# Random-feature attention, MLP and capacity-routed experts on one core: accumulator hand-over, low parts kept on chip and load order around the range check

## The chip, the cores and the metric

The kernel runs on one core of a Trainium2 chip, as one program. The metric is the device time of one execution in microseconds (us), taken as the median of several runs. A core has TensorE (PE; its weight loads are listed apart as PEld), VectorE (DVE), ScalarE (ACT), GpSimd (POOL) and SyncE (SP, which here issues most DMA transfers).

## The reference

Three layers follow each other over 2304 tokens (4 batches of 576, 8 heads of 64, so 512 features a token), all in float32:

```python
q_p, k_p = phi(q*scale), phi(k*scale)      # exp(x@omega.T - |x|^2/2 - max) / sqrt(128)
x = (q_p @ (k_p.T @ v)) / (q_p @ k_p.sum(seq) + 1e-6)         # per batch and head
h = x @ w_in; x = (h - tanh(h)) @ w_out                       # 512 -> 2048 -> 512
logits = x @ w_gate                                           # 8 experts
for idx in argsort(-logits.flatten()):                        # greedy, 288 tokens an expert at most
    tok, e = idx // 8, idx % 8
    if assigned[tok] < 0 and counts[e] < 288: assigned[tok] = e; counts[e] += 1
for e in range(8):
    out[assigned == e] = relu(x[assigned == e] @ w1[e]) @ w2[e]   # 512 -> 1024 -> 512
```

## The kernel before, in words

**Precision.** A float32 product is made of three fast matmuls: each operand is split into a high part H and a low part L (line 298 copies the high part, line 303 subtracts it to give the low one), and H·H, H·L and L·H are added in PSUM. The names end in H and L accordingly: `xH`/`xL` the tokens, `gH`/`gL` the hidden values, `iL` and `oL` the low parts of `w_in` and `w_out`, which are kept in DRAM and loaded chunk by chunk (L563).

**Blocks and chunks.** The MLP runs over 6 blocks of 384 tokens. A block has 16 chunks of 128 hidden features: 12 first matmuls a chunk (L601 to L603), a polynomial for h − tanh h on ACT and DVE (L605, L625 to L628), the split into `gH` and `gL`, and 9 second matmuls a chunk (`m2_ops`, L648; below "m2"), three for each of the block's three token tiles, into three accumulators in PSUM, `acc0` to `acc2` (the ring `accr`).

**The last two blocks.** Blocks 4 and 5 go through the first half together, chunk by chunk. Block 5's first matmuls use the same three accumulators as their PSUM room, while block 4's use the four-bank ring `bank`. A shortcut replaces their m2 in the gate: `last_logits` gets the logits from `gH`, `gL` and the precomputed product w_out·w_gate (L719, L721), and L732 and L736/L737 transpose and add them. Block 4's `gH` stay in the place of the used `w_in` chunk (`wi`); its `gL` go to DRAM (L800) and come back for the m2 (L822), through a ring of four slots. Block 5's `gH` and `gL` (`gH5`, `gL5`) stay on chip.

**The range check.** The polynomial holds for a limited range. All engines read one flag (L1464) and branch (L1465); the branch's body, which computes everything again with tanh, is not entered with these inputs. Block 4's m2 for its first three chunks (27 m2) stand ahead of the check, the other 117 behind it, then block 5's 144 (`last_ops`).

**Routing and experts.** Behind the check the capacity search for the experts begins: DVE forms masks (L992 to L996, L1035), PE counts them (nine small matmuls, L1041), DVE decides (L1060, L1062), PE spreads the decision (L1066), and so on, threaded between the m2; L1198 and L1205 give the list of expert 0's tokens, L1161 starts the next expert. Expert 0's tokens are gathered and transposed (L1311); those that lie in the last block are picked by a selection matrix from that block's own results `mH`/`mL` (L1315). Then come the experts' matmuls (L1339 to L1341 by w1, L1358 to L1360 by w2), whose weights are loaded as 512 KB pieces (`wraw`, L1254 and L1257), the high part on ACT, the low part from DRAM (L1266) or by subtraction.

**Order.** A `Plan` object records each operation with its engine, a cost and a due time (`plan.at`), takes its dependences from the buffers that it reads and writes (`op`), and then emits the program engine by engine in the planned order. So an edit of a due time, of a ring of buffers, or of a dependence changes the order on all engines.

## Time and profile before

| what | value |
|---|---|
| median of 3 runs | 907.14 us (904.26 to 910.89) |
| the profiled execution | 907.36 us |
| span of its instructions | 905.5 us |
| TensorE busy | 866.9 us, 96% of the span |
| VectorE, ScalarE, GpSimd busy | 651.0, 467.1, 251.9 us |
| mean granted TensorE clock | 0.980 of full speed |
| DMA traffic | 194.72 MB, 215 GB/s in the mean |

The span runs from the first to the last instruction; 1.86 us of the execution's time lie around it. All positions below are us from the start of the span. The range check lies at 544.5, block 4's last m2 at 582.6, block 5's at 628.1; from there on the experts run. A duration listed for a matmul is from its start to its modelled end; consecutive matmuls overlap, so that their pace is read from their starts.

### The profile page before, as it was taken

The page shows a single profiled execution, that of the slowest core. Times are in us where ns is not written, and L with a number is a line of the kernel's source. Part 1 is how long each engine was busy: PE and PEld are TensorE (multiplying, and loading weights), DVE is VectorE, ACT ScalarE, POOL GpSimd, SP SyncE. Part 2 cuts the span into 40 slices and gives each one's busy share as a digit, 9 for nine tenths or more (in the row PEclk, how much of TensorE's full clock was granted, in tenths as well). Part 3 has the DMA queues.
Part 4 walks back from the last instruction along what each step waited for, and adds up shares of the span by engine and source line. Part 5 has one row for each costly group of instructions (what it writes and reads, how often), then busy time and mean ns, then how long its engine had stood idle before and what let it go on. Part 6 is the DMA issues. An engine that isn't in the chain of part 4 may idle for free. (4 is left out here: it accounts for less than half of the span.)

```text
span 905.5 us, 17561 instructions
## 1 busy us (share of the span) xinstructions
PE 866.9 (96%) x6168; PEld 770.9 (85%) x6168; DVE 651.0 (72%) x1933; ACT 467.1 (52%) x1015; POOL 251.9 (28%) x272
## 2 busy tenths in 40 slices
...
GB/s 245 345 270 270 273 235 282 275 226 224 116 221 166 206 201 225 176 101 111 158 318 259 273 192 176 229 196 132 236 265 260 283 219 232 266 191 278 215 28 26
DMA packets 104364, 194.72 MB, mean 215 GB/s; under 512 B 28369, under 2 KB 42833, under 8 KB 104274
## 3 DMA queue, kind: packets, MB, share of 16 engines
...
## 5 line engine op out<-in xcount | busy, mean ns | idle before, releaser
L601 PE MATMUL bk<-xH,wi 128*128 128x384 f32 x320 | 114.0, 356 | 1.6 <-DVE xt L500 1.3
L648 PE MATMUL acc<-wo,gL 128*128 128x512 f32 x288 | 114.6, 400 | 0.0
L602 PE MATMUL bk<-xL,wi 128*128 128x384 f32 x320 | 107.9, 337 | 0.5 <-DVE xL L303 0.5
L603 PE MATMUL bk<-xH,iL 128*128 128x384 f32 x320 | 107.9, 337 | 0.0
L707 DVE SCALAR_TENSOR_TENSOR lw<-wf,raw 128x512 f32<-128x512 f32 x128 | 105.4, 824 | 2.9 <-POOL wf L704 1.4
L648 PE MATMUL acc<-wo,gH 128*128 128x512 f32 x240 | 100.2, 417 | 0.0
L303 POOL TENSOR_TENSOR gL<-s,gH 128x384 fp32r<-128x384 f32 x52 | 62.0, 1193 | 137.0 <-ACT gH L298 137.0
L648 PE MATMUL acc<-oL,gH 128*128 128x512 f32 x240 | 95.8, 399 | 0.3 <-DVE oL L303 0.3
L438 ACT ACTIVATE phi<-bk,nm 128x128 f32<-128x128 f32 x272 | 76.9, 379 | 36.1 <-DVE nm L441 35.5
L704 POOL TENSOR_TENSOR wf<-oL,wo 128x512 f32<-128x512 f32 x48 | 65.6, 1366 | 70.5 <-DMA oL<-low_wo 65.9
L626 DVE SCALAR_TENSOR_TENSOR s<-s,bk 128x384 f32<-128x384 f32 x80 | 44.0, 550 | 43.7 <-ACT s L625 43.0
L298 ACT ACTIVATE gH<-s 128x384 fp32r<-128x384 f32 x80 | 42.2, 527 | 62.1 <-DVE s L628 46.9
L601 PEld LDWEIGHTS bk<-xH,wi 128*128 128x128 f32 x320 | 60.6, 189 | 7.1 <-issue 1.5
L648 PEld LDWEIGHTS acc<-wo,gL 128*128 128x128 f32 x288 | 54.7, 190 | 12.7
L602 PEld LDWEIGHTS bk<-xL,wi 128*128 128x128 f32 x320 | 60.7, 190 | 3.3 <-DVE xL L303 0.7
L605 ACT ACTIVATE u<-bk 128x384 f32<-128x384 f32 x80 | 39.1, 488 | 43.7 <-PE bk L603 42.5
L603 PEld LDWEIGHTS bk<-xH,iL 128*128 128x128 f32 x320 | 60.4, 189 | 0.0
L441 DVE TENSOR_REDUCE nm<-bk 128x4 f32<-128x512 f32 (+1 forms) x75 | 46.5, 633 | 14.3 <-PE bk L427 13.2
L628 DVE SCALAR_TENSOR_TENSOR s<-s,u 128x384 f32<-128x384 f32 x80 | 52.8, 660 | 1.1
L648 PEld LDWEIGHTS acc<-wo,gH 128*128 128x128 f32 x240 | 45.5, 189 | 6.8
L625 ACT ACTIVATE s<-u,qbias 128x384 f32<-128x384 f32 x80 | 49.3, 616 | 3.8 <-DVE gL L303 1.4
L648 PEld LDWEIGHTS acc<-oL,gH 128*128 128x128 f32 x240 | 45.5, 190 | 6.6 <-DVE oL L303 0.6
...
## 6 DMA issues: line engine op xcount, KB each, us to landing
...
```

Source lines behind the costliest of these rows:

```text
L303: (nc.gpsimd if e == POOL else nc.vector).tensor_tensor(out, in_, high.bitcast(F32), op=OP.subtract)
L438: nc.scalar.activation(ph.t[:, i0 + i, :], pj.t[:, i * M:(i + 1) * M], AF.Exp, bias=nmx.t[:, i0 + i:i0 + i + 1])
L441: plan.op(DVE, 0.1 + 0.125 * n, lambda e, pj=pj, i0=i0, n=n: V.tensor_reduce(nmx.t[:, i0:i0 + n], pj.t[:, :n * M].rearrange("p (i m) -> p ...
L601: nc.tensor.matmul(ph(), piece(iH, c), xH.t[:, c, :], start=(c == 0), stop=False)
L602: nc.tensor.matmul(ph(), piece(iH, c), xL.t[:, c, :], start=False, stop=False)
L603: nc.tensor.matmul(ph(), piece(iL, c), xH.t[:, c, :], start=False, stop=(c == NC - 1))
L625: plan.op(ACT, 0.52, lambda e: nc.scalar.activation(s.t, ut(), AF.Square, bias=qbias), r=[u], w=[s], lag=2.8)
L626: plan.op(DVE, 0.52, lambda e: V.scalar_tensor_tensor(s.t, s.t, QD, ph(), op0=OP.add, op1=OP.mult), r=[p, s], w=[s], lag=3.4)
L628: plan.op(DVE, 0.65, lambda e: V.scalar_tensor_tensor(s.t, s.t, QC, ut(), op0=OP.mult, op1=OP.mult), r=[u, s], w=[s], lag=4.0)
L648: nc.tensor.matmul(acc[t].t, (gL if k == 2 else gH).t[:, c], (oL if k == 1 else oH).t, start=(f == 0 and k == 0), stop=(f == NF - 1 and k ...
L704: plan.op(POOL, 1.45, lambda e: nc.gpsimd.tensor_tensor(w.t, lo.t.bitcast(F32), wo[:, f, :].bitcast(F32), op=OP.add), r=[lo, wbuf["wo", f] ...
L707: x_reads.append(plan.op(DVE, 0.9, lambda e, i=i: nc.vector.scalar_tensor_tensor(scratch.t.bitcast(F32), w.t, 1.0, half(rows[i // 2], i % ...
```

## The change

1. `Plan.op` gets partial reads and writes (`rp`, `wp`): the three or four pieces of `xH`/`xL`, and of the experts' `xgH`/`xgL`, are no longer ordered against each other as whole tiles.
2. Block 5's first matmuls for its last three chunks take their PSUM room from `bank` and no longer from `accr`, and block 4's first m2 wait for block 5's chunk 12 (`freed`) instead of its last chunk.
3. For block 4's last two chunks, 14 and 15 (`NKEEP`), `gL` stays on chip in two new buffers (`gLk0`, `gLk1`), and their `oL` are loaded early into two slots of the ring `xm`. They are the first two chunks behind the check, and accumulation ends at chunk 13 (`end`).
4. Expert 0's weight loads are tied to block 5's loads of `oL` (`turn`, `oloads`), one piece per chunk at the earliest. Three of the eight freed `wi` places go to the experts' low parts, and the slot counts `SLOTS` follow.
5. Block 5's last three chunks (`ALONE`) are done token tile by token tile, so that the tiles end one after the other; the fourth bank of expert 0's transposes takes `acc1`, and `switch3`, which hands the accumulators to the experts, moves behind expert 0.
6. On the path for out-of-range inputs, one ring has one slot less and two buffers are written in one step. These instructions are not executed here.

Where an operation may go to POOL or to DVE, the plan decides anew: of the 32 splits of the experts' w1 that are made ahead of the check (`dw`, L303), POOL has ten instead of six, the last five of them in the place of its last three.

The diff, cut to its core (lines left out give `op` its new parameters, add the ring `keptr` with two tiles, and cast `xm`, which is now stored as the matmuls' type):

```diff
-        for b in w:
+        for b in (*w, *wp):
             if b.ring is not None:
                 o.new.append(b)
                 if not b.writers:
                     b.ring.order.append((o.prio, b))
-            o.deps.update(b.readers)
+            if b in w:
+                o.deps.update(b.readers)
             b.writers.append(o)
-        for b in r:
+        for b in (*r, *rp):
...
-        plan.op(ACT, 0.48, lambda e: copy(e, part(xH), pv()), r=[tp], w=[xH], lag=0.6)
-        plan.op(DVE, 0.6, lambda e: low(e, part(xL), pv(), part(xH)), r=[tp, xH], w=[xL], lag=1.3)
+        o = plan.op(ACT, 0.48, lambda e: copy(e, part(xH), pv()), r=[tp], wp=[xH], lag=0.6)
+        plan.op(DVE, 0.6, lambda e: low(e, part(xL), pv(), part(xH)), r=[tp], rp=[xH], wp=[xL], after=[o], lag=1.3)
...
-        p, u, s = Buf(accr if alone else bank), Buf(gHr if alone else ur), Buf(sr)
+        p, u, s = Buf(accr if alone and f < NF - TPB else bank), Buf(gHr if alone else ur), Buf(sr)
...
-    def m2_ops(f, g, wsp, acc, prev, fine=False):
+    def m2_ops(f, g, wsp, acc, prev, fine=False, end=NF - 1, tiles=range(TPB)):
...
-        for t in range(TPB):
+        for t in tiles:
...
-                                     start=(f == 0 and k == 0), stop=(f == NF - 1 and k == 2), skip_group_check=True)
+                                     start=(f == 0 and k == 0), stop=(f == end and k == 2), skip_group_check=True)
...
+            if f == NF - TPB - 1:
+                freed[:] = flags[-1:]
...
-            gH, gL = Buf(None, wi[:, f, :BLK]), Buf(gLr)
+            stay = f >= NF - NKEEP
+            gH, gL = Buf(None, wi[:, f, :BLK]), None if stay else Buf(gLr)
             gH.readers = list(wbuf["wi", f].readers)
+            if stay:
+                gL, oL = kept.setdefault(f, (Buf(keptr), Buf(xmr)))
+                at, plan.at = plan.at, start[j] + 20.0
+                plan.op(SP, 0.47, lambda e, f=f, oL=oL: nc.sync.dma_start(oL.t.bitcast(F32), lows["wo", f]), w=[oL],
+                        after=[stored_low["wo", f]], nbytes=P * DM * 4)
+                plan.at = at
             hidden_ops(s4, gH, gL)
             lprev4 = last_logits(j, lacc4, f, lprev4, gH, gL)
-            g4[f] = gH, plan.op(SP, 0.47, lambda e, f=f, gL=gL: nc.sync.dma_start(g4l[f], gL.t.bitcast(F32)), r=[gL],
-                                nbytes=P * BLK * 4, lag=6.8)
+            g4[f] = gH, None if stay else plan.op(
+                SP, 0.47, lambda e, f=f, gL=gL: nc.sync.dma_start(g4l[f], gL.t.bitcast(F32)), r=[gL],
...
-        but_last_ops(0, NHERE, start[j] + step[j] * NF + 1.0, 2.0)
-
-    g4, acc4, prev4 = {}, [], [None]
+        for b in kept_bufs() if not general else ():
+            b.left += 1
+        but_last_ops(range(NHERE), start[j] + step[j] * NF + 1.0, 2.0)
+
+    g4, acc4, prev4, freed = {}, [], [None], []
...
-    def but_last_ops(f0, f1, start, step):
-
-        for f in range(f0, f1):
-            plan.at = start + step * f
...
+    kept_bufs = lambda: [b for f in sorted(kept) for b in kept[f]]
+
+    def but_last_ops(chunks, start, step):
+
+        for i, f in enumerate(chunks):
+            plan.at = start + step * i
             gH, st = g4[f]
-            gL = Buf(gLr)
-            plan.op(SP, 0.47, lambda e, f=f, gL=gL: nc.sync.dma_start(gL.t.bitcast(F32), g4l[f]), w=[gL], after=[st],
-                    nbytes=P * BLK * 4)
-            prev4[0] = m2_ops(f, (gH, gL), split_ops("wo", f), acc4, prev4[0] if f else [flags[-1]] * TPB)
-
-    stored, stored4, m5 = [], [], []
+            if st:
+                gL = Buf(gLr)
+                plan.op(SP, 0.47, lambda e, f=f, gL=gL: nc.sync.dma_start(gL.t.bitcast(F32), g4l[f]), w=[gL], after=[st],
+                        nbytes=P * BLK * 4)
+                oH, oL = split_ops("wo", f)
+            else:
+                (gL, oL), oH = kept[f], wbuf["wo", f]
+            prev4[0] = m2_ops(f, (gH, gL), (oH, oL), acc4, prev4[0] if f else freed * TPB, end=NF - NKEEP - 1)
+
+    stored, stored4, m5, oloads = [], [], [], []
+    ALONE = 3
...
+        wsp = []
         for f in range(NF):
             plan.at = start + step * f
-            prev = m2_ops(f, g5[f], split_ops("wo", f), acc, prev, True)
+            wsp.append(split_ops("wo", f))
+            oloads.append(wsp[f][1].writers[-1])
+            if f < NF - ALONE:
+                prev = m2_ops(f, g5[f], wsp[f], acc, prev, True)
         for t in range(TPB):
+            for f in range(NF - ALONE, NF):
+                plan.at = start + step * (NF - ALONE + (f - NF + ALONE + ALONE * t) / TPB)
+                prev = m2_ops(f, g5[f], wsp[f], acc, prev, True, tiles=[t])
+        for t in range(TPB):
+            plan.at = -60.0
             hi, lo = Buf(mHr), Buf(mLr)
             plan.op(ACT, 0.48, lambda e, hi=hi, t=t: copy(e, hi.t, acc[t].t), r=[acc[t]], w=[hi])
             plan.op(DVE, 0.6, lambda e, hi=hi, lo=lo, t=t: low(e, lo.t, acc[t].t, hi.t), r=[acc[t], hi], w=[lo])
...
-    SLOTS = {"wraw": (3, 4), "ewH": (0, 4), "ewL": (1, 11), "xg": (NG - 1, NG - 1), "xgH": (1, 2), "xgL": (1, 2),
+    SLOTS = {"wraw": (3, 4), "ewH": (0, 7), "ewL": (1, 8), "xg": (NG - 1, NG - 1), "xgH": (1, 2), "xgL": (1, 2),
...
-            plan.op(SP, 0.47, load, w=[raw], after=[o], nbytes=P * FX * 4)
+            turn = [] if p else [oloads[min(2 * i + 2, NF - 1)]]
+            plan.op(SP, 0.47, load, w=[raw], after=[o] + turn, nbytes=P * FX * 4)
...
-                plan.op(SP, 0.47, load_low, w=[L], after=[o], nbytes=P * FX * 4)
+                turn = [] if p else [oloads[2 * i + 3]]
+                plan.op(SP, 0.47, load_low, w=[L], after=[o] + turn, nbytes=P * FX * 4)
...
-        plan.at = base + AT_TURN if p else -58.0
         for c in range(NC):
-            tp = Buf(bank3)
+            plan.at = base + AT_TURN if p else -58.0 if c < NC - 1 else AT_LAST + AT_W * NF
+            tp = Buf(accr if c == NC - 1 and not p else bank3)
...
                 o = plan.op(PE, 0.38, others, r=xg, w=[tp])
+                plan.at = AT_LAST + AT_W * NF + 5.0
...
-            plan.op(ACT, 0.3, lambda e, c=c, tp=tp: copy(e, xH.t[:, c], tp.t[:, :CAP]), r=[tp], w=[xH])
-            plan.op(DVE, 0.37, lambda e, c=c, tp=tp: low(e, xL.t[:, c], tp.t[:, :CAP], xH.t[:, c]), r=[tp, xH], w=[xL])
+                plan.at = -58.0
+            o = plan.op(ACT, 0.3, lambda e, c=c, tp=tp: copy(e, xH.t[:, c], tp.t[:, :CAP]), r=[tp], wp=[xH])
+            xs_[c] = plan.op(DVE, 0.37, lambda e, c=c, tp=tp: low(e, xL.t[:, c], tp.t[:, :CAP], xH.t[:, c]),
+                             r=[tp], rp=[xH], wp=[xL], after=[o])
+            if tp.ring is accr:
+                end_ops.extend(plan.ops[n0:])
...
-    but_last_ops(NHERE, NF, AT_LAST - 1.5 * NF, 1.5)
-    for b in acc4:
+    for b in acc4 + kept_bufs():
         b.left -= 1
+    but_last_ops([*range(NF - NKEEP, NF), *range(NHERE, NF - NKEEP)], AT_LAST - 1.5 * (NF - NHERE), 1.5)
...
-        rings["ewH"].add(Places(), [str(2 * i) for i in range(NF // 2)], t=now)
+        for i in range(NF // 2):
+            rings["ewL" if i in (2, 4, 6) else "ewH"].add(Places(), [str(2 * i)], t=now)
...
-    plan.op("-", 0.0, switch3, after=end_ops)
...
+            if not p:
+                plan.op("-", 0.0, switch3, after=end_ops)
```

**TensorE ahead of the check.** These rows stand before the change, where block 5's chunk 15 ends and the logits of chunk 13 come; block 4's chunk 15 stands just ahead of them; the names `wi` in second place are block 4's `gH`.

```order
L601 MATMUL acc0_1401<-xH1_5524,wi_118 128x384
L602 MATMUL acc0_1401<-xL1_5535,wi_118 128x384
L603 MATMUL acc0_1401<-xH1_5524,iL1_6345 128x384
L648 MATMUL acc1_1408<-wo_119,wi_118 128x512
L648 MATMUL acc1_1408<-oL0_5494,wi_118 128x512
L648 MATMUL acc1_1408<-wo_119,gL3_5776 128x512
L648 MATMUL acc1_1408<-wo_119,wi_118 128x512
L648 MATMUL acc1_1408<-oL2_5542,wi_118 128x512
L648 MATMUL acc1_1408<-wo_119,gL1_5824 128x512
L719 MATMUL kv0_5689<-gH5_13_6492,vgs_117 16x384
L721 MATMUL kv0_5689<-gL5_13_6498,vgs_117 8x384
```

After the change this stands at the same chunk 15 of block 5 (now in `bk3`).

```order
L605 MATMUL bk3_6517<-xH1_5528,iL1_6350 128x384
L603 MATMUL bk3_6517<-xH1_5528,wi_118 128x384
L604 MATMUL bk3_6517<-xL1_5539,wi_118 128x384
L605 MATMUL bk3_6517<-xH1_5528,iL1_6350 128x384
L650 MATMUL acc0_1401<-wo_119,wi_118 128x512
L650 MATMUL acc0_1401<-oL2_5546,wi_118 128x512
L650 MATMUL acc0_1401<-wo_119,gL0_5820 128x512
L650 MATMUL acc1_1408<-wo_119,wi_118 128x512
L650 MATMUL acc1_1408<-oL1_5606,wi_118 128x512
L650 MATMUL acc1_1408<-wo_119,gL3_5891 128x512
L650 MATMUL acc2_1413<-wo_119,wi_118 128x512
```

Before, all 27 m2 stood behind the last first-layer matmul; now 15 of them stand ahead of it, 3 between the first matmuls of chunks 13 and 14, 12 between those of chunks 14 and 15, and 12 behind it.

**TensorE behind the check.** Before, the branch is followed by the nine counting matmuls, whose last two and what follows them are these rows.

```order
L1041 LDWEIGHTS pairs0_11790
L1041 MATMUL rp0_11819<-r_cmp1_11809,pairs0_11790 40x62
L1066 LDWEIGHTS d8_987
L1066 MATMUL rp1_11837<-id8_985,d8_987 128x8
L648 MATMUL acc1_1408<-wo_119,wi_118 128x512
L648 MATMUL acc1_1408<-oL1_11800,wi_118 128x512
L648 MATMUL acc1_1408<-wo_119,gL0_11796 128x512
```

After the change the branch is followed by m2 of chunk 14, with `xm1` as `oL` and `gLk0` as `gL`.

```order
L1507 UNCONDITIONAL_BRANCH x2
L650 MATMUL acc1_1408<-wo_119,wi_118 128x512
L650 MATMUL acc1_1408<-xm1_2107,wi_118 128x512
L650 MATMUL acc1_1408<-wo_119,gLk0_6523 128x512
L650 MATMUL acc2_1413<-wo_119,wi_118 128x512
L650 MATMUL acc2_1413<-xm1_2107,wi_118 128x512
L650 MATMUL acc2_1413<-wo_119,gLk0_6523 128x512
```

The counting matmuls now stand behind 12 m2, and L1099 (L1066 before) behind 6 more.

**TensorE at the end of block 5.** Before, the last m2 of `acc0` are mixed with the first selection matmuls.

```order
L648 MATMUL acc2_1413<-oL0_12636,gH5_15_6573 128x512
L648 MATMUL acc2_1413<-wo_119,gL5_15_6582 128x512
L1315 MATMUL bd0_12451<-r_sel0_12313,mH0_12700 128x288
L1315 MATMUL bd1_12457<-r_sel0_12313,mH0_12700 128x288
L1315 MATMUL bd2_12461<-r_sel0_12313,mH0_12700 128x288
L648 MATMUL acc0_1401<-wo_119,gH5_15_6573 128x512
L1130 LDWEIGHTS onesb_975
L1130 MATMUL rp0_12739<-r_M0_12726,onesb_975 128x36
L1131 LDWEIGHTS tri_973
L1131 MATMUL rp0_12739<-r_M0_12726,tri_973 128x36
L648 MATMUL acc0_1401<-oL0_12636,gH5_15_6573 128x512
L648 MATMUL acc0_1401<-wo_119,gL5_15_6582 128x512
```

After the change `acc2` ends here, then come the gathered tokens' transposes into `acc1`, and nine m2 of `acc0`, of which these are the first two.

```order
L650 MATMUL acc2_1413<-wo_119,gL5_14_6574 128x512
L650 MATMUL acc2_1413<-wo_119,gH5_15_6599 128x512
L650 MATMUL acc2_1413<-oL2_12586,gH5_15_6599 128x512
L650 MATMUL acc2_1413<-wo_119,gL5_15_6601 128x512
L1099 LDWEIGHTS d8_987
L1099 MATMUL rp1_12689<-id8_985,d8_987 128x8
L1347 MATMUL acc1_1408<-ident_99,r_xg0_12301 128x128
L1347 MATMUL acc1_1408<-ident_99,r_xg1_12318 128x128
L1347 MATMUL acc1_1408<-ident_99,xg_rest_11792 128x128
L650 MATMUL acc0_1401<-wo_119,gH5_13_6506 128x512
L650 MATMUL acc0_1401<-oL1_12533,gH5_13_6506 128x512
```

The selection matmuls (now L1351) all stand behind `acc0`'s last m2, 24 of them, and behind these at once expert 0's first (now L1380); the steps of the next expert's routing that stood there before (L1161, L1162, nine of L1041) come later.

**SyncE's loads for expert 0.** Before, four pieces stand between the loads of chunks 0 and 1 of `oL`.

```order
L563 DMA oL0_12185<-low_wo0_136 128x512
L1254 ISA
L1254 DMA r_wraw0_12193<-in_moe2_w1_dram 128x1024
L1266 ISA
L1266 DMA r_ewL0_12198<-w1l_80 128x1024
L1254 ISA
L1254 DMA r_wraw1_12206<-in_moe2_w1_dram 128x1024
L1254 ISA
L1254 DMA r_wraw2_12213<-in_moe2_w1_dram 128x1024
L563 DMA oL2_12221<-low_wo1_137 128x512
```

After the change the first pieces stand behind chunk 4's load.

```order
L565 DMA oL1_12254<-low_wo4_140 128x512
L1287 ISA
L1287 DMA r_wraw0_12282<-in_moe2_w1_dram 128x1024
L1300 ISA
L1300 DMA r_ewL0_12306<-w1l_80 128x1024
L1287 ISA
L1287 DMA r_wraw1_12321<-in_moe2_w1_dram 128x1024
L565 DMA oL0_12336<-low_wo5_141 128x512
L565 DMA oL2_12354<-low_wo6_142 128x512
L565 DMA oL1_12367<-low_wo7_143 128x512
```

The rest follows in the same way: two pieces each behind chunks 7 and 12, one each behind 9 and 15.

## Rows read from the trace of the kernel before

**Rows 1.** Busy time by stretch, core 0: from:to, length, PE, PEld, DVE, ACT, POOL, clock, DMA share, GB/s.
```profile
528.00:544.70 16.70, 12.67 (x53) 7.53 (x51) 10.75 (x22) 9.07 (x18) 5.82 (x5) 0.90 0.43 166
544.70:549.80 5.10, 0.73 (x11) 0.58 (x11) 2.50 (x10) 0.00 (x0) 1.89 (x4) 0.61 0.58 169
549.80:582.60 32.80, 32.80 (x181) 24.00 (x181) 15.77 (x84) 1.06 (x2) 0.00 (x0) 0.96 0.60 187
582.60:590.00 7.40, 4.30 (x42) 2.65 (x40) 5.14 (x27) 3.33 (x5) 0.00 (x0) 1.00 0.99 355
590.00:593.90 3.90, 3.90 (x18) 2.65 (x17) 1.59 (x6) 0.46 (x1) 0.46 (x1) 0.56 0.90 351
593.90:628.10 34.20, 34.20 (x196) 25.80 (x193) 12.08 (x67) 4.15 (x6) 2.53 (x3) 1.00 0.38 113
628.10:634.50 6.40, 4.60 (x37) 3.70 (x36) 5.89 (x22) 3.49 (x8) 0.98 (x1) 1.00 0.82 298
634.50:638.00 3.50, 3.50 (x18) 3.35 (x16) 3.44 (x13) 2.00 (x2) 0.69 (x1) 0.51 1.04 304
638.00:872.00 234.00, 232.95 (x2024) 217.73 (x2024) 167.38 (x724) 123.36 (x205) 58.03 (x80) 1.00 0.76 232
```

**Rows 2.** The same for TensorE instructions of L648 alone, in two of the stretches.
```profile
549.80:552.40 2.60, 2.60 (x6) 0.50 0.88 284
597.00:609.00 12.00, 10.96 (x47) 1.00 0.44 134
```

**Rows 3.** TensorE's timeline around the check: start, length, operation, idle time before it and releaser.
```profile
527.88 0.33 PE L603 MATMUL acc<-xH,iL 128*128 128x384 f32 x1
534.27 0.50 PE L648 MATMUL acc<-wo,wi 128*128 128x512 f32 x1 [1.75 <-DVE s L626]
548.51 0.65 PE L1041 MATMUL rp<-r_cmp,pairs 128*40 128x62 bf16 x9 [4.41 <-DVE pairs L996]
549.73 0.19 PE L1066 MATMUL rp<-id,d 128*128 128x8 bf16 x1 [0.56 <-DVE r_cond L1062]
549.77 0.78 PE L648 MATMUL acc<-wo,wi 128*128 128x512 f32 x1
```

**Rows 4.** VectorE's timeline: last instruction before the check, first one after it.
```profile
544.36 0.18 DVE L737 TENSOR_TENSOR lg<-lg,bk 128x24 f32<-128x24 f32 x1
546.19 0.30 DVE L992 TENSOR_REDUCE r_m<-lg 128x18 f32<-128x144 f32 x1 [1.66 <-DVEq L1465]
```

**Rows 5.** POOL's timeline before the check.
```profile
525.04 1.60 POOL L303 TENSOR_TENSOR dw<-dw,dh 128x512 fp32r<-128x512 f32 x1 [9.81 <-ACT dh L298]
534.57 1.11 POOL L303 TENSOR_TENSOR gL<-s,wi 128x384 fp32r<-128x384 f32 x1 [2.44 <-DMA g4l<-gL]
541.21 1.00 POOL L303 TENSOR_TENSOR gL<-s,wi 128x384 fp32r<-128x384 f32 x1 [1.34 <-PE acc L648]
```

**Rows 6.** VectorE's timeline before the check: line L628 twice.
```profile
525.41 1.65 DVE L628 SCALAR_TENSOR_TENSOR s<-s,u 128x384 f32<-128x384 f32 x1
527.56 0.56 DVE L628 SCALAR_TENSOR_TENSOR s<-s,gH 128x384 f32<-128x384 f32 x1
```

**Rows 7.** TensorE's timeline at the start of block 5.
```profile
586.24 0.17 PE L1161 MATMUL rp<-onesb,r_gs 128*8 128x1 bf16 x1 [0.56 <-DVE r_gs L1156]
588.47 0.51 PE L1041 MATMUL rp<-r_cmp,pairs 128*40 128x62 bf16 x9 [1.98 <-DVE pairs L996]
```

**Rows 8.** SyncE's timeline: the load of chunk 1's low part of w_out.
```profile
580.94 0.37 SPq L563 DMA_DIRECT2D oL<-low_wo  x1
```

**Rows 9.** TensorE's weight loads: the one that waits for that load.
```profile
590.00 0.19 PEld L648 LDWEIGHTS acc<-oL,gH 128*128 128x128 f32 x1 [0.26 <-DMA oL<-low_wo]
```

**Rows 10.** TensorE's timeline from block 5's last matmul to expert 0's first.
```profile
627.84 0.40 PE L648 MATMUL acc<-wo,gL 128*128 128x512 f32 x1
631.53 0.44 PE L1311 MATMUL bd<-ident,r_xg 128*128 128x128 f32 x2 [0.73 <-DVE r_xgL L303]
634.49 0.57 PE L1339 MATMUL bd<-r_xgH,wi 128*128 128x288 f32 x1
```

32 lines of the change are left out of this document (19 added, 13 removed).

## Prediction

> **What bounds the kernel now.** The stretches come first [rows 1]. From 638 to 872, in the experts, TensorE is busy 232.95 of 234.00 us at a clock of 1.00, and in 549.8 to 582.6 and 593.9 to 628.1 it is busy all the time. So TensorE is the bound, and time can be won where it stands still or runs at the lower of its two levels. The table shows four such places around the change. 528.0 to 544.7, ahead of the check: 12.67 of 16.70 us busy. 544.7 to 549.8, behind it: 0.73 of 5.10. 582.6 to 590.0, at block 5's start: 4.30 of 7.40. 628.1 to 634.5, between block 5 and expert 0: 4.60 of 6.40. Behind the last three the granted clock falls (0.96 in the mean of one stretch, 0.56 and 0.51 in two), which is the level of 1.2 GHz instead of 2.4 for a few us. What that costs is read from the m2 alone [rows 2]: 2.60 us for 6 at 0.50, 10.96 for 47 at 1.00, so 0.433 against 0.233 us each. Then the timelines of the four places say who is waited for [rows 3 to 10]. What is won before 638 passes through, since the experts behind it are bound by TensorE, and every step of the sum is a gain of TensorE.
>
> **A. Ahead of the check.** The last first-layer matmul starts at 527.88 and VectorE's last instruction ahead of the branch ends at 544.36 + 0.18 = 544.54 [rows 3, 4]. In between no engine is full: VectorE 10.75, ScalarE 9.07, POOL 5.82 of 16.70 us [rows 1]. It is a chain of waits. The first m2 there waits 1.75 us for an accumulator that VectorE still reads [rows 3]; POOL's split of `gL` waits 2.44 us for a store to DRAM and, at 541.21, 1.34 us for an m2, both times for a slot of the ring of four [rows 5]. Parts 2 and 3 of the change take these away: the accumulators come free by chunk 12, 15 of the 27 m2 move ahead of chunk 15, and chunks 14 and 15 have buffers of their own. The 15 m2 put the last first-layer matmul 15 × 0.233 = 3.5 us later, to 531.6. From there at the least one chunk's six operations, two on VectorE of 0.56 us [rows 6], three on ScalarE taken as long as these, one on POOL of 1.11 [rows 5], 3.9 us together (estimate), and then what follows the last `gL`, 544.54 − 542.21 = 2.3: 537.8, a gain of 6.7. If the backlog of the polynomial stays as it is, nothing is gained, and 0.5 may be lost to `bank`, whose room for chunk 14's second half is given by chunk 13's first half, only 27 matmuls earlier. I take the two waits of POOL (the 1.75 lies beside the first of them), 3.8, less 0.8 for that room: **3.0** (−0.5 to 6.7).
>
> **B. Behind the check.** TensorE now waits 4.41 us for `pairs` and 0.56 for the decision [rows 3]; of the 5.10 us 4.4 are idle. Afterwards 12 m2 come first whose inputs all lie on chip, so only the branch is left: VectorE needs 1.66 us for it [rows 4]; TensorE has no row of its own, and I take 1.1 (0.5 to 1.7). VectorE has `pairs` 548.51 − 544.54 = 4.0 us after the last instruction; the 12 m2 cover 2.8 us of that at the full clock and 5.2 at the lower one, which they will have, as now [rows 2]. The decision is covered by 6 m2. Gain 4.4 − 1.1 = **3.3** (2.2 to 3.9). The dip of the clock I count as unchanged.
>
> **C. Start and course of block 5.** Removed: 7.40 − 4.30 = 3.1 us of waits (1.98 for `pairs`, 0.56 each for `r_gs` and for the decision are the main ones [rows 7, 3]), 0.2 for `oL` [rows 9], and 8 m2 at the lower clock, 8 × 0.2 = 1.6: 4.9. Added: at four places the decision now stands directly behind the counting matmuls, each 0.56 [rows 3], 2.2. And SyncE's queue: chunk 5's `oL` now stands behind three pieces of 512 KB, chunks 8 and 13 behind two, chunk 10 behind one. SyncE works in order, so each piece whose slot is not yet free holds the `oL` behind it too. At the 355 GB/s of 582.6 to 590.0 [rows 1], 1.75 MB take 4.9 us; a load is issued about two chunks ahead, 18 × 0.233 = 4.2 us, so chunk 5 is 0.7 late and nothing else. By the other row, the load at 580.94 behind 2 MB is awaited until 590.00 [rows 8, 9], 9.1 us for 2.25 MB, chunk 5 is 2.8 late and chunks 8 and 13 0.8 each, 4.4. I take 2.4, since 113 GB/s in 593.9 to 628.1 leave room. C: 4.9 − 2.2 − 2.4 = **0.3** (−6 to 4.9).
>
> **D. From block 5 to expert 0.** Now 634.49 − 628.07 = 6.4 us from the end of the last m2's turn to the first expert matmul, with 0.73 in one wait for a transposed low part to give its bank back [rows 10], nine counting matmuls and two waits for masks; then 3.50 us at 0.51 [rows 1], 1.7 lost. Afterwards two tiles are finished under the nine m2 of `acc0`, the fourth bank is `acc1`, and the counting comes later. Left are 24 selection matmuls at 4.60/37 = 0.124, 3.0 us, about 0.4 for `acc0`'s copy, 0.9 for the last transposes' two copies: 4.3, and 0.4 for the three transposes that now stand ahead: 4.7. Gain 1.7, and of the clock's 1.7 I take 1.3, since the idle pieces become short: **3.0** (0.7 to 3.6).
>
> **E. The rest.** Partial reads (part 1) reorder block boundaries and expert loads. Where TensorE is the bound that moves nothing: **0** (−1.5 to 1.5), covered by the same busy TensorE; without that cover it would be the 0.56 of a single wait at each of a few places.
>
> Sum: 3.0 + 3.3 + 0.3 + 3.0 = 9.6 us from the profiled execution's 907.36 (span 905.5 and 1.86 around it): 897.8. The median shown is 0.2 lower: 897.6.
>
> **The rivals.** *The check does not come earlier.* One VectorE instruction beside POOL's `dw` split takes 1.65 us where it takes 0.56 alone [rows 5, 6], so 1.1 more. In POOL's order ten of these splits stand in the place of six, the last five after the point where three stood before. Five such holds are 5.5 us in the chain of A and eat its 3.0; if all fall on the chain, 0.5 to 2.5 are lost beside it: about 901.5. Against it: four of the six before left no trace on the chain. The Trainium skill, page "SBUF — State Buffer", section "SBUF: two separate sides", says that a VectorE instruction with two inputs in SBUF and a GpSimd instruction that reads SBUF hold a shared pair of ports as an exclusive lock, one blocking for the whole of the other. The trace agrees (1.65 beside 1.60), and the rule speaks for this rival: by it every one of the five can cost a whole instruction.
>
> *Slower: the expert's loads starve block 5.* If all three batches of two or three pieces bring their `oL` as late as the load at 580.94, 9.1 us after its issue with 4.2 covered, each costs 4.9 us, three 14.7; C becomes 4.9 − 2.2 − 14.7 = −12.0, the sum 3.0 + 3.3 − 12.0 + 3.0 = −2.7, and the time 910. It decides once these stalls exceed the 9.6 of the sum. For it: 355 GB/s in the one place where the pieces stand together now. Against: they are spread, and at 113 GB/s the transfers there are far from full.
>
> *More: the stalls are all covered.* No late `oL`, decisions covered, and A at 5: C 2.7, sum 14.0, 893.3.
>
> *The tail does not do what it says.* The first group of expert 0 now needs all four pieces of w1, the fourth standing behind chunk 9's `oL`. If one of them or its low part is late by 3 us, D is gone: 900.6.
>
> **How the numbers follow.** Forecast 0.55 (own range 893.5 to 901), check not earlier 0.15, more 0.13, tail 0.10, slower 0.07. The range reaches from the rival with more and A's far end, 889, to 906, ahead of the starved case. A measurement of this kernel tells about 1% from no change, 9.1 us, so faster means below 898.1: somewhat over half of the forecast and the case with more, 0.46. Slower, above 916.2, is the worse part of the starved case and what I do not see: 0.05. The rest, 0.49, lies within 1%.
>
> **What would show it.** A: VectorE's last instruction ahead of the branch near 541.5, and no wait of POOL for a store. B: m2 about 1 us behind it, no wait for `pairs`. C: no idle stretch at block 5's start, but waits for `oL` of chunks 5, 8 or 13 and four of 0.56. D: under 5 us from the last m2 to L1380 at a clock near 1. Wrong it would be if the check stands at 544 or later, if the m2 behind it wait for a reloaded `gL`, or if block 5 loses over 5 us to its loads.

## The result, and the profile after

The changed kernel takes 897.51 us in the median of 18 runs (894.73 to 906.51), the kernel before 907.11 (903.12 to 916.73, 18 runs): a ratio of 0.9905, 95% interval 0.9885 to 0.9926. The forecast was 897.6. The profiled execution is 897.55 long with a span of 895.7 (before 905.5). The total was met; of the terms behind it A and E were not, and C and D only in part.

The stretches of the kernel after answer to [rows 1]: start of blocks 4 and 5, last first-layer matmul to check, behind the check up to block 5, block 5 in three pieces, its end to expert 0, expert 0's start, experts.

```profile
core 0: us, PE busy (x) PEld busy (x) DVE busy (x) ACT busy (x) POOL busy (x), PEclk, DMA share, GB/s
459.42:468.64 9.22, 7.33 (x36) 6.11 (x34) 6.83 (x15) 6.71 (x14) 2.61 (x2) 0.81 0.65 224
535.80:545.30 9.50, 6.85 (x34) 3.93 (x32) 7.62 (x13) 4.46 (x10) 5.60 (x4) 1.00 0.46 175
545.30:579.50 34.20, 33.90 (x188) 24.44 (x189) 14.54 (x77) 1.13 (x2) 1.89 (x4) 0.95 0.55 165
579.50:593.00 13.50, 12.50 (x80) 9.30 (x78) 8.70 (x45) 2.78 (x4) 2.99 (x3) 1.00 0.91 306
593.00:598.00 5.00, 3.39 (x19) 2.68 (x19) 1.78 (x7) 0.00 (x0) 0.00 (x0) 1.00 0.85 290
598.00:625.50 27.50, 26.22 (x155) 18.57 (x154) 13.02 (x64) 6.30 (x8) 0.98 (x1) 1.00 0.64 191
625.50:629.00 3.50, 3.50 (x27) 3.18 (x26) 3.42 (x17) 2.04 (x5) 0.00 (x0) 1.00 0.27 89
629.00:632.50 3.50, 3.50 (x26) 3.31 (x26) 3.46 (x12) 3.46 (x6) 0.80 (x1) 1.00 1.04 400
632.50:866.50 234.00, 234.00 (x2056) 220.56 (x2055) 170.34 (x737) 124.72 (x207) 57.96 (x81) 1.00 0.75 228
```

The idle stretch behind the check is gone, block 5 starts without one but has a hole at 593 to 598, expert 0 starts at the full clock, and the experts' 234 us have no idle time where they had 1.05. The last 9.5 us ahead of the check are still a chain of waits: TensorE is idle for 2.65 of them.

**How the runs are compared.** From the first H·H matmul of the first layer to the start of block 4 the same work takes 385.6 to 390.6 us in the profiled executions of this study, so the text measures from there. The marks are: *start* (the 257th H·H matmul of the first layer, the first of blocks 4 and 5, which go together), the *25th* H·H matmul counted from it, the *last* one, the *check* (end of VectorE's last instruction ahead of the branch), *block 5* (first m2 with `gH5`), *expert 0* (its first matmul) and the *end* of the span. Lengths in us, from the timelines, each from one profiled execution; the last column is the median time.

```
kernel        start-25th  25th-last  last-check  check-blk5  blk5-expert  expert-end    time
before          22.69       64.29      17.00       38.04       51.91        271.0      907.1
after           25.82       67.92       9.81       34.23       49.53        266.7      897.5
x_blocks        25.83       67.93       9.81       34.06       51.82        267.1      897.3
no_bank         25.77       63.69      16.46       33.78       52.31        267.0      901.1
no_keep         22.69       68.46       9.79       39.52       45.48        269.6      898.2
no_alone        25.56       68.26      10.32       34.27       53.64        267.2      899.7
late_keep       22.69       71.45       9.39       34.11       49.98        266.5      896.9
late_keep_dw    22.07       72.19       7.03       34.23       51.69        266.5      895.8
dw_dve          23.16       67.32       9.54       34.84       49.71        266.3      894.7
no_spread       25.81       67.91       9.80       34.10       51.93        268.5      900.8
dw_gather       24.71       67.21       9.54       34.81       50.61        268.1      897.1
gather_late     25.82       67.93       9.81       34.00       50.39        268.4      898.7
b_dw_dve        22.07       63.90      15.47       39.49       52.66        269.1      904.6
x_experts       25.69       68.13      10.32       34.21       52.06        266.7      901.5
```

The 95% interval of after's ratio overlaps or touches that of each of its variants, so that the lengths carry the argument; all the times of no_bank and x_experts lie above after's median, all those of dw_dve below it. And each edit lets the plan decide anew: POOL makes ten splits of `dw` in after, eight in no_bank, no_keep and late_keep, none where the edit says so.

The span fell by 9.8: 0.4 up to the check (103.98 to 103.55), 3.8 from it to block 5, 2.4 in block 5 and its end, 4.3 in the experts, less 1.1 by which this execution reached the start later.

**Behind the check.** VectorE's last instruction and its first one behind the branch, of after; they answer to [rows 4].

```profile
545.06 0.18 DVE L739 TENSOR_TENSOR lg<-lg,bk 128x24 f32<-128x24 f32 x1
546.89 0.30 DVE L1025 TENSOR_REDUCE r_m<-lg 128x18 f32<-128x144 f32 x1 [1.65 <-DVEq L1507]
```

TensorE's timeline there, which answers to [rows 3].

```profile
543.12 0.34 PE L723 MATMUL bk<-gLk,vgs 128*8 128x384 f32 x1 [1.01 <-POOLq L1507]
545.60 0.67 PE L650 MATMUL acc<-wo,wi 128*128 128x512 f32 x1 [0.80 <-PEq L1507]
546.07 0.63 PE L650 MATMUL acc<-xm,wi 128*128 128x512 f32 x1
...
549.78 0.39 PE L650 MATMUL acc<-wo,gLk 128*128 128x512 f32 x1
550.10 0.44 PE L1074 MATMUL rp<-r_cmp,pairs 128*40 128x62 bf16 x9
```

VectorE ends at 545.06 + 0.18 = 545.24; the first m2 follows 0.36 us later (5.23 before), while VectorE needs 1.65 for the same branch. There is no wait for `pairs` any more. The first m2 still run at the lower clock, 0.43 us each up to 549.

**Block 5.** All of TensorE's waits between 579 and 605; two more like the third follow, 0.56 and 0.61 us.

```profile
584.10 0.61 PE L1231 MATMUL rp<-r_ohh,r_lid 128*32 128x18 bf16 x18 [0.19 <-DVE r_lid L1224]
584.96 0.17 PE L1238 MATMUL rp<-r,spread 128*128 128x18 bf16 x1 [0.26 <-DVE r L1236]
592.77 0.18 PE L1099 MATMUL rp<-id,d 128*128 128x8 bf16 x1 [0.56 <-DVE r_cond L1095]
593.98 0.33 PE L1347 MATMUL bd<-ident,r_xg 128*128 128x128 f32 x1 [0.87 <-DMA r_xg<-ms,r_ix]
595.05 0.33 PE L1347 MATMUL bd<-ident,xg_rest 128*128 128x128 f32 x1 [0.74 <-DMA xg_rest<-ms,r_ix]
```

No load of `oL` is waited for. The second and the third gather of expert 0's tokens are, 1.6 us together; the first has landed when TensorE comes to it at 592.81. POOL issues the three in the timeline at 586.87 to 589.59, and the view of DMA issues (584 to 600) gives how long they are under way, beside an `oL` load.

```profile
586.87 1.15 POOL L1329 DMA_INDIRECT r_xg<-ms,r_ix  x1 [39.37 <-DVE r_a L1026]
588.32 0.96 POOL L1329 DMA_INDIRECT r_xg<-ms,r_ix  x1 [0.30 <-issue]
589.59 0.88 POOL L1329 DMA_INDIRECT xg_rest<-ms,r_ix  x1 [0.30 <-issue]
```

```profile
oL<-low_wo SPq DMA_DIRECT2D x5, 256.0 KB, 2.7
r_xg<-ms,r_ix POOLq DMA_INDIRECT x2, 5.5
xg_rest<-ms,r_ix POOLq DMA_INDIRECT x1, 5.4
```

**Tail.** TensorE from block 5's last m2 to expert 0, which answers to [rows 10]; then VectorE's low parts of expert 0's tokens.

```profile
625.24 0.40 PE L650 MATMUL acc<-wo,gL 128*128 128x512 f32 x1
...
628.77 0.29 PE L1351 MATMUL acc<-r_sel,mL 128*128 128x288 f32 x1
629.00 0.40 PE L1380 MATMUL bd<-r_xgH,wi 128*128 128x288 f32 x1
629.24 0.29 PE L1381 MATMUL bd<-r_xgL,wi 128*128 128x288 f32 x1
```

```profile
628.49 1.19 DVE L305 TENSOR_TENSOR r_xgL<-bd,r_xgH 128x288 fp32r<-128x288 f32 x3
629.59 0.45 DVE L305 TENSOR_TENSOR r_xgL<-acc,r_xgH 128x288 fp32r<-128x288 f32 x1
```

From the end of the last m2's turn to expert 0 it is 629.00 − 625.47 = 3.53 us, 6.42 before. The expert's first products stand at 629.00, a microsecond ahead of the end of the last low part, 629.59 + 0.45 = 630.04: the matmuls that read the first quarters no longer wait for the last.

### The profile page after: what moved, and what is told of

Read it like the earlier page. It is cut to its first block, busy times and chain, and to the rows that moved or that the text cites. A ratio compares the mean times of both kernels' runs of the same rounds, so it can differ in the third digit from the quotient of the medians.

```text
span 895.7 us, 17533 instructions
## 1 busy us (share of the span) xinstructions
PE 863.1 (96%) x6168; PEld 768.8 (86%) x6168; DVE 657.8 (73%) x1931; ACT 467.6 (52%) x1017; POOL 252.5 (28%) x272
## 5 line engine op out<-in xcount | busy, mean ns | idle before, releaser
L603 PE MATMUL bk<-xH,wi 128*128 128x384 f32 x332 | 118.3, 356 | 1.6 <-DVE xt L502 1.0
L604 PE MATMUL bk<-xL,wi 128*128 128x384 f32 x332 | 111.9, 337 | 0.5 <-DVE xL L305 0.5
L605 PE MATMUL bk<-xH,iL 128*128 128x384 f32 x332 | 112.1, 338 | 0.0
L650 PE MATMUL acc<-wo,gL 128*128 128x512 f32 x282 | 111.7, 396 | 0.0
L709 DVE SCALAR_TENSOR_TENSOR lw<-wf,raw 128x512 f32<-128x512 f32 x128 | 108.1, 844 | 2.2 <-POOL wf L706 1.0
L628 DVE SCALAR_TENSOR_TENSOR s<-s,bk 128x384 f32<-128x384 f32 x83 | 45.6, 550 | 37.1 <-ACT s L627 36.8
L603 PEld LDWEIGHTS bk<-xH,wi 128*128 128x128 f32 x332 | 62.9, 190 | 8.4 <-PE bk L482 1.3
L604 PEld LDWEIGHTS bk<-xL,wi 128*128 128x128 f32 x332 | 63.0, 190 | 3.3 <-DVE xL L305 0.7
L650 PEld LDWEIGHTS acc<-wo,gL 128*128 128x128 f32 x282 | 52.9, 188 | 12.6 <-POOL gL L305 0.3
L605 PEld LDWEIGHTS bk<-xH,iL 128*128 128x128 f32 x332 | 62.6, 189 | 0.0
L630 DVE SCALAR_TENSOR_TENSOR s<-s,u 128x384 f32<-128x384 f32 x80 | 54.6, 682 | 1.2
```

Of the source, the lines that this page charges most:

```text
L603: nc.tensor.matmul(ph(), piece(iH, c), xH.t[:, c, :], start=(c == 0), stop=False)
L604: nc.tensor.matmul(ph(), piece(iH, c), xL.t[:, c, :], start=False, stop=False)
L605: nc.tensor.matmul(ph(), piece(iL, c), xH.t[:, c, :], start=False, stop=(c == NC - 1))
L628: plan.op(DVE, 0.52, lambda e: V.scalar_tensor_tensor(s.t, s.t, QD, ph(), op0=OP.add, op1=OP.mult), r=[p, s], w=[s], lag=3.4)
L630: plan.op(DVE, 0.65, lambda e: V.scalar_tensor_tensor(s.t, s.t, QC, ut(), op0=OP.mult, op1=OP.mult), r=[u, s], w=[s], lag=4.0)
L650: nc.tensor.matmul(acc[t].t, (gL if k == 2 else gH).t[:, c], (oL if k == 1 else oH).t, start=(f == 0 and k == 0), stop=(f == end and k == ...
```

## The experiments

Theory and rivals at the start: the forecast's terms A to E, and its rival that the check does not come earlier. The first four kernels undo one part each.

**x_blocks.** Part 1 undone in the blocks, kept in the experts.

```diff
-         o = plan.op(ACT, 0.48, lambda e: copy(e, part(xH), pv()), r=[tp], wp=[xH], lag=0.6)
-         plan.op(DVE, 0.6, ..., r=[tp], rp=[xH], wp=[xL], after=[o], lag=1.3)
+         plan.op(ACT, 0.48, lambda e: copy(e, part(xH), pv()), r=[tp], w=[xH], lag=0.6)
+         plan.op(DVE, 0.6, ..., r=[tp, xH], w=[xL], lag=1.3)
```

> The changed kernel with the block tokens' pieces (xH, xL) ordered as whole tiles again; the experts' pieces stay partial. By the trace of the changed kernel TensorE comes 4 us late to the last chunks, 1.1 us before 440 and 2.9 us between 455 and 470, where it idles 1.7 us and drops to the lower clock. Theory: part 1 of the change costs this, and the check moves with it; then this kernel takes 893.5 to 895 us and VectorE's last instruction ahead of the branch ends near 541.5. Rival: the chain on VectorE, ScalarE and POOL sets the check and takes up the 4 us; then 897.5 within 1 us and the end near 545.

897.27 us, ratio 0.9879 (0.9833 to 0.9926), and the same lengths as after up to block 5. The theory falls, the rival stands: partial reads in the blocks give nothing that can be measured. The 2.3 us more in block 5 are longer waits for the gathers (2.3 us in two places, 1.6 in after) and a mean granted clock of 0.97 instead of 1.00 there.

**no_bank.** Part 2 undone: block 5's last chunks take the accumulators' banks again, and block 4's m2 wait for its last chunk.

```diff
-         p, u, s = Buf(accr if alone and f < NF - TPB else bank), ...
+         p, u, s = Buf(accr if alone else bank), ...
-             if f == NF - TPB - 1:
+             if f == NF - 1:
```

> The changed kernel with part 2 undone: block 5's last chunks in the accumulators again, block 4's first m2 free only after the last chunk. Theory: the early release is what made up for the lateness ahead of the check, so the check comes 3 to 4 us later than in the changed kernel, about 901 us. Rival: with buffers of their own for chunks 14 and 15 the 27 m2 are no longer in the chain and fill its gaps wherever they stand, and the room in bank was only a new wait; then 896.5 to 898.

901.09 us, 0.9933 (0.9904 to 0.9963). From start to check 105.92 us, 2.4 more than after. TensorE waits again as in [rows 3]:

```profile
536.62 0.34 PE L723 MATMUL bk<-gL,vgs 128*8 128x384 f32 x1 [1.80 <-DVE gL L305]
538.18 0.63 PE L650 MATMUL acc<-wo,wi 128*128 128x512 f32 x1 [1.22 <-DVE s L628]
```

Last-check goes back to 16.46. So the early accumulators shorten the stretch behind the last first-layer matmul, as term A has it. POOL's two waits of [rows 5], for a store and for an m2, are there again as well, though chunks 14 and 15 keep their own buffers:

```profile
538.60 1.37 POOL L305 TENSOR_TENSOR gL<-s,wi 128x384 fp32r<-128x384 f32 x1 [2.92 <-DMA g4l<-gL]
544.27 1.16 POOL L305 TENSOR_TENSOR gL<-s,wi 128x384 fp32r<-128x384 f32 x1 [4.30 <-PE acc L650]
```

The median agrees with the theory (about 901), but only 2.4 of its 3 to 4 us are at the check; block 5 and its end are 2.8 us longer, up to its last m2 at a granted clock of 0.93.

**no_keep.** Part 3 undone: no low part stays on chip.

```diff
-     NKEEP, kept = 2, {}
+     NKEEP, kept = 0, {}
```

> The changed kernel with part 3 undone (no low parts kept; chunk order 3 to 15 behind the check). Theory: behind the branch nothing but the routing is ready, TensorE waits about 4 us more there, and the last gL wait for stores again: 901 to 903 us, the first m2 5 us behind VectorE's last instruction. Rival: the reload of the first chunks was hidden by the counting anyway and the plan puts m2 first all the same; then 898 to 899.

898.24 us, 0.9895 (0.986 to 0.993): in the sum no different from after, by very different terms. Behind the check the old picture is back:

```profile
545.52 0.65 PE L1074 MATMUL rp<-r_cmp,pairs 128*40 128x62 bf16 x9 [4.41 <-DVE pairs L1029]
...
546.78 0.77 PE L650 MATMUL acc<-wo,wi 128*128 128x512 f32 x1
```

The first m2 comes 5.23 us behind the check, and block 5 5.3 us later behind it than in after. But the check comes 3.0 us earlier than before (100.94), and block 5 is 4.1 us shorter than after's. POOL asks for the gathers at 586.29 and TensorE comes to them at 595.13, 8.8 us later, where in after it comes 5.9 us later (592.81 behind 586.87) and waits. Nor does TensorE wait for a decision there: its longest wait in block 5 is 0.20 us, and up to the last m2 it is idle for 0.45 us, in after for 3.89. So the kept low parts (part 3) give 5.3 us behind the check, cost 2.6 ahead of it, and hand 4.1 back in block 5, 1.6 for the gathers and most of the rest for decisions and the list of tokens, which TensorE now reaches before they are ready. In the experts the kernel without them is 2.9 us longer. The theory's 5 us behind the check are there; its time of 901 to 903 is not.

**no_alone.** Part 5 undone: block 5's last chunks not tile by tile, and `bank3` for the fourth transposes.

```diff
-     ALONE = 3
+     ALONE = 0
...
-             tp = Buf(accr if c == NC - 1 and not p else bank3)
+             tp = Buf(bank3)
```

> The changed kernel with part 5 undone (block 5's last chunks over all three tiles, fourth transposes in the ring of banks, accumulators handed over before expert 0). Theory: 6 us again from the last m2 to the first expert matmul in place of 3.5, and 3.5 us at the lower clock behind it: 901 to 902 us. Rival: what was won there is the later place of the routing steps and comes from the loads; then 898 to 899.

899.66 us, 0.9921 (0.9891 to 0.995). The last m2 to expert 0 takes 4.63 us (3.53 in after, 6.42 before), with the old wait for a bank:

```profile
627.39 0.40 PE L1349 MATMUL bd<-r_sel,mL 128*128 128x288 f32 x1 [0.24 <-DVE mL L305]
630.00 0.44 PE L1345 MATMUL bd<-ident,r_xg 128*128 128x128 f32 x2 [0.72 <-DVE r_xgL L305]
```

So part 5 carries 1.1 of the 2.9 us at the tail, between the theory, which gave it nearly all, and the rival, which gave it none; what carries the rest is shown by x_experts below. Block 5 up to its last m2 is 3.0 us longer than in after (48.78 to 45.77): the waits for gathers are 2.5 in place of 1.6, and the granted clock is 0.97 in place of 1.00. That this is the edit's doing is not shown.

**Where term A went.** In the table, after loses 3.1 us between the start and the 25th matmul, almost 80 us ahead of the check and where the forecast had not looked. TensorE's two waits there, where it is idle for 1.9 us in place of 0.9, then VectorE's and POOL's instructions just ahead:

```profile
460.78 0.34 PE L723 MATMUL kv<-gL,vgs 128*8 128x384 f32 x1 [1.02 <-DVE mm L899]
...
463.04 0.44 PE L603 MATMUL acc<-xH,wi 128*128 128x384 f32 x1 [0.72 <-ACT xm L300]
```

```profile
457.79 1.77 DVE L305 TENSOR_TENSOR dw<-dw,dh 128x512 fp32r<-128x512 f32 x1
...
460.65 0.13 DVE L899 TENSOR_SCALAR mm<-mm 1x1 f32<-1x1 f32 x1
```

```profile
457.43 1.58 POOL L305 TENSOR_TENSOR dw<-dw,dh 128x512 fp32r<-128x512 f32 x1
```

The second wait is followed by the lower clock (the stretch 459.42 to 468.64 has 0.81). SyncE's timeline shows that the loads of the two kept `oL` went out long before:

```profile
153.23 0.33 SPq L806 DMA_DIRECT2D xm<-low_wo  x1
167.78 0.37 SPq L806 DMA_DIRECT2D xm<-low_wo  x1
```

They hold two slots of the ring `xm` from then on. Two suspects: these slots, and VectorE held beside POOL (1.77 where the same split takes 0.67 to 0.69 alone in this stretch).

**late_keep.** The two loads wait for the gate of block 3.

```diff
+                 gates[:] = plan.ops[-1:]
...
-                         after=[stored_low["wo", f]], nbytes=P * DM * 4)
+                         after=[stored_low["wo", f], *gates], nbytes=P * DM * 4)
```

> The changed kernel, with the two kept oL loaded only behind block 3's gate. In the changed kernel they are issued at 153 and 168 us and hold two of the three xm slots from there to the check, and TensorE waits for xm at the block boundaries; without kept low parts those waits are gone and VectorE's last instruction ahead of the branch ends at 541.55 in place of 545.24. Theory: the lateness ahead of the check is these slots, not part 1 of the change; then the end near 541.5, the first m2 0.4 us behind it, and 893 to 894.5 us in all. Rival: the chain on VectorE, ScalarE and POOL behind the boundary takes up what is won; then the end at 544 or later and 897 us.

896.85 us, 0.9888 (0.9865 to 0.9911). The loads now go out at 468.17, and up to the 25th matmul the kernel has the pace of before (22.69): with the slots held this stretch is longer, which no_keep shows too. But the check is no earlier (103.53): the rival stands. That VectorE's last instruction ends at 541.02, where the theory had it, is no gain, since this execution reached the start 4.2 us before after's. The planner puts the matmuls behind in another order, in which the last first-layer matmul stands as late as in after (22.69 + 71.45 = 94.14, against 93.74): 18 m2 stand ahead of it in place of 15, and between the 25th and the check TensorE is idle for 4.9 us, in no_keep for 3.2.

**late_keep_dw and dw_dve.** The low part of `dw` always on VectorE, in late_keep and in after.

```diff
-                 plan.op({POOL: 1.45, DVE: 0.65}, 0, lambda e, raw=raw, hi=hi, h=h: low(
+                 plan.op(DVE, 0.65, lambda e, raw=raw, hi=hi, h=h: low(
```

> As late_keep, and the splits of the experts' w1 (dw) all on VectorE instead of ten of them on POOL. In the changed kernel five instructions of VectorE ahead of the check take about 1.65 us beside POOL's in place of 0.56. Theory: these 5.5 us lie on the chain, so without POOL's dw the check comes 2 to 3 us earlier than in late_keep: 890.5 to 892. Rival: VectorE takes over ten splits of 0.69, 6.9 us, and other splits on POOL (gL) hold it as well; then within 1 us of late_keep or later.

895.75 us, 0.9872 (0.9848 to 0.9897); start to check 101.29, 2.2 less than late_keep. So the theory's 2 to 3 us are there at the check, its time of 890.5 to 892 is not: block 5 and its end are 1.7 us longer again.

> The changed kernel with the splits of the experts' w1 (dw) all on VectorE. Theory (VectorE held beside POOL is on the chain ahead of the check): VectorE's last instruction ahead of the branch near 542.5 in place of 545.24, 895 us. Rival (TensorE's lateness sets the check): 545, 897.5 us.

894.69 us, 0.9856 (0.9827 to 0.9885), the lowest time of the study, as the theory had it; start to check 100.02, 3.5 less than after. But the table says where: 2.7 of the 3.5 are won before the 25th matmul, 0.6 up to the last one, and only 0.3 behind it. VectorE is held five times in after's last 25 us (1.37 to 1.67 us), which is what the forecast's rival rested on; in dw_dve three holds of 1.30 to 1.37 us remain there, beside POOL's splits of `gL`, and VectorE has the low parts of `dw` to make as well. The net of all this is the 0.3. What a single hold costs there was not measured.

**no_spread.** Part 4's ties undone: expert 0's pieces are loaded as soon as they have a slot.

```diff
-             turn = [] if p else [oloads[min(2 * i + 2, NF - 1)]]
+             turn = []
```

> The changed kernel with expert 0's loads no longer tied to block 5's oL loads (slots as changed). Theory: the pieces go out together as soon as their slots are free and hold up oL loads at block 5's start: one wait for oL of 2 to 4 us there and a spell at the lower clock behind it, 899 to 901 us. Rival: the spread only moved the loads, since 100 to 250 GB/s leave room: 897.5 within 1 us.

900.83 us, 0.9917 (0.9883 to 0.995). In block 5 a wait of 1.92 us for `pairs` comes, no wait for `oL`:

```profile
591.95 0.31 PE L1074 MATMUL rp<-r_cmp,pairs 128*40 128x62 bf16 x5 [1.92 <-DVE pairs L1029]
```

So the theory's time was met, but not by its wait. The clock there is 0.93 in the mean. Since no_bank has 0.93 in block 5 too, without this edit, the clock's part need not be the edit's, and the intervals of no_spread and after overlap: what the ties are worth stays open, between nothing and 3 us.

**dw_gather.** dw_dve, and expert 0's transposes 17 m2 later.

```diff
-                 r=[ix], w=[t], after=stored if p else stored4, late=5.0)
+                 r=[ix], w=[t], after=stored if p else stored4, late=5.0 if p else 9.0)
```

> Two edits on the changed kernel: the low part of dw is always split on VectorE, and expert 0's gathered tokens are first needed about 17 m2 later (their transposes into acc1 move behind 17 more m2 of block 5). Theory: the gains add, 3.5 us ahead of the check (from the start of block 4 to VectorE's last instruction 100 us instead of 103.5) and 1.6 us of waits for the gathers in block 5 (from its start to expert 0's first matmul 48 instead of 49.5): 892.5 to 893. Rival: the 1.6 us come back at another place (a wait at the tail, since the transposes' copies now lie nearer to the end, or for the next gather), and the time is that of the kernel with dw on VectorE alone, 894.7 within 1.

897.07 us, 0.9903 (0.9866 to 0.9939): the gains do not add. It shows two things. The first is in the stretches 21 to 24 us behind the start, of dw_dve and then of dw_gather (columns PE, PEld, DVE, ACT, POOL, clock, DMA share, GB/s):

```profile
464.33:467.33 3.00, 3.00 (x21) 2.79 (x20) 2.87 (x5) 2.28 (x5) 1.44 (x1) 1.00 0.95 353
```

```profile
460.34:463.34 3.00, 3.00 (x11) 2.63 (x10) 2.87 (x5) 2.01 (x4) 1.44 (x1) 0.51 0.95 341
```

Both have the same wait of 0.72 us just ahead. Behind it one granted 1.00 and the other 0.51, and this is their difference of 1.55 us up to the 25th matmul. So of the 2.7 us that dw_dve won there, 1.55 are the clock's, and 1.1 go with POOL's splits. Whether the clock falls there does not look like chance alone: in the profiled executions of this study in which TensorE is idle for 1.9 us between the start and the 25th matmul it falls, seven of seven; in those with 0.45 to 0.96 us, in one of seven. The second is in block 5: the wait for gathers is gone, and in its place TensorE waits for `oL`.

```profile
590.82 0.50 PE L650 MATMUL acc<-oL,gH 128*128 128x512 f32 x1 [1.39 <-DMA oL<-low_wo]
```

**gather_late.** The second edit alone, on after.

> One edit on the changed kernel: the transposes of expert 0's gathered tokens into acc1 stand 17 m2 (4 us) later. Theory: the two waits for gathered rows that have not landed, 0.87 and 0.74 us, go, since the rows land 2 us at most after they were asked for; block 5's start to expert 0's first matmul 48 us or less instead of 49.5, the time 895.5 to 896. Rival: the gathers are slow because the loads take the bandwidth, and what is won there is lost at the tail: 49.5 again and 897.5.

898.67 us, 0.9912 (0.9886 to 0.9938); block 5 50.39. The theory fell. The rival stands in so far as nothing was won, but the loss is in block 5 and not at the tail:

```profile
592.25 0.50 PE L650 MATMUL acc<-oL,gH 128*128 128x512 f32 x1 [0.46 <-DMA oL<-low_wo]
...
594.64 0.50 PE L650 MATMUL acc<-oL,gH 128*128 128x512 f32 x1 [0.74 <-DMA oL<-low_wo]
```

1.2 us of waits for loads have taken the place of 1.6 for gathers. At 306 GB/s over its first 13.5 us, the start of block 5 has a transfer that is late in after, dw_gather and gather_late; that the bandwidth is the reason is likely, but was not tested by itself. The experts are also 1.7 us longer than after's; where was not followed.

**b_dw_dve.** The `dw` edit on the kernel before.

> One edit on the kernel before: the low part of dw is always split on VectorE. Theory (the holds are a price that the change's own order raises): the kernel before has one hold of 1.1 us in the last 25 us ahead of the check, so from block 4's start to VectorE's last instruction 103 to 104 us, as before, and 906 to 907. Rival: POOL's dw costs this kernel too, all along the blocks, and the gain is the same 3 us as in the changed kernel: 100.5 to 101 us and 904.

904.62 us, 0.9987 (0.9959 to 1.0015): no difference shown by the times; in the profile 2.5 us fewer up to the check (101.44). The marks are nearer to the rival (100.5 to 101) than to the theory (103 to 104). So without POOL's splits of `dw` the kernel before gains 2.5, after 3.5, and the holds alone do not explain what the change lost.

**x_experts.** Part 1 undone in the experts alone: the products wait for all of `xgH` and `xgL`.

```diff
-             o = plan.op(ACT, 0.3, ..., r=[tp], wp=[xH])
+             o = plan.op(ACT, 0.3, ..., r=[tp], w=[xH])
...
-                 o = plan.op(PE, 0.40, mm, r=[H, L], rp=[xH, xL], w=[ph], after=[xs_[c]] + ([o] if o else []))
+                 o = plan.op(PE, 0.40, mm, r=[xH, xL, H, L], w=[ph], after=[o] if o else [])
```

> One edit on the changed kernel: the partial reads and writes are undone in the experts alone (a product of the bank ph again waits for all of xH and xL). Theory: the 4.3 us that the experts became shorter come in part from these: from expert 0's first matmul to the end 268 to 270 us instead of 266.7, the time 899 to 901. Rival: they come from the clock, the spread loads and the gathers' place, and the partial reads give nothing: 266.7 within 0.5 and 897.5 within 1.

901.51 us, 0.9941 (0.9918 to 0.9964), 4.0 more than after. Expert 0 to the end takes 266.7 us as in after, so the rival was right about the place; yet the time is nearer to the theory's. From start to end the profiled execution is 3.1 us longer than after's, and 2.8 of them are at the tail:

```profile
627.18 0.29 PE L1351 MATMUL acc<-r_sel,mL 128*128 128x288 f32 x1
627.83 0.17 PE L1194 MATMUL rp<-onesb,r_gs 128*8 128x1 bf16 x1 [0.35 <-DVE r_gs L1189]
...
629.23 0.31 PE L1074 MATMUL rp<-r_cmp,pairs 128*40 128x62 bf16 x5 [1.14 <-DVE r_cmp L1068]
629.92 0.37 PE L1074 MATMUL rp<-r_cmp,pairs 128*40 128x62 bf16 x4 [0.38 <-DVE r_cmp L1068]
630.22 0.61 PE L1380 MATMUL bd<-r_xgH,wi 128*128 128x288 f32 x1
```

The last m2's turn ends at 623.88, so 6.34 us to expert 0 instead of 3.53: with whole tiles the expert's first product is not ready, the planner puts the next expert's counting ahead of it, and TensorE waits for VectorE's masks. Behind the idle pieces the expert's first matmuls are at the lower clock (0.24 us apart up to 633, instead of 0.13), as before the change.

## Why the prediction was right, and where it was wrong

**The total** was right to 0.1 us by luck, because errors cancelled: A was 2.6 too high and C 0.8, the experts gave 2.6 beside the clock where E had nothing, B, D and the clock gave 2.1 more than forecast, and the profiled execution had lost 1.1 earlier. Two slips of the prediction change nothing in its sum: 527.88 + 3.5 is 531.4, not 531.6; and in the rival *more*, with the decisions covered, C is 4.9 and not 2.7, the time about 891, from which the range's 889 follows.

**A, predicted 3.0, measured 0.4.** The size of what it looked at was right: the last first-layer matmul stands 3.6 us later against its predecessors for the 15 m2 (64.29 to 67.92; forecast 3.5), last-check falls from 17.00 to 9.81 (forecast 541.5 − 531.4 = 10.1), and no_keep, which has part 2 without part 3, comes 3.0 us earlier in the sum. Of the mechanism one half is wrong. The term was priced by POOL's two waits, which parts 2 and 3 together were to end; part 3's own buffers are not needed for that. no_keep, without them, has last-check 9.79 and no such wait behind the last first-layer matmul; no_bank, with them, has 16.46 and both. Part 2 carries the term. What failed in the sum is a term that the prediction does not have. Part 3's early loads were given no price, and E, which did look at block boundaries, looked at part 1, which x_blocks shows to cost nothing there; nor is TensorE busy all the time at that place, as E's cover has it. The two early `oL` loads take slots of `xm` from 153 us on, the start of blocks 4 and 5 is planned otherwise, and 3.1 us go there. That the slots begin it is shown by no_keep and late_keep, which have before's 22.69. But dw_dve, with the slots held, has 23.16: dw_gather and dw_dve put 1.1 down to POOL's splits beside VectorE and about 1.5 to the lower clock behind the wait, so that either edit takes nearly all of it away. Why late_keep does not gain the 3 us at the check is open; its order differs all along.

**The rival "the check does not come earlier"** had the check nearly right (0.4 us earlier), and its time of 901.5 and the place wrong. It put five holds of 1.1 us into the last 25 us. They are there (four of 1.1 and one of 0.8), but last-check is as short as the forecast had it without them (9.81 against 10.1), and dw_dve, which has three others in their place, wins only 0.3 there; what went lost went at the start of blocks 4 and 5. The rule that it cites of the Trainium skill, page "SBUF — State Buffer", section "SBUF: two separate sides", agrees with the trace in each hold (1.77 beside POOL's 1.58 at 457); what neither the rule nor a hold's length tells is whether the chain runs through it.

**B, predicted 3.3, measured 3.8.** TensorE's branch was taken as 1.1 us; it starts 0.36 behind VectorE's last instruction. The dip of the clock stayed, as forecast.

**C, predicted 0.3, measured −0.5.** The removed waits are gone and the clock is 1.00 at block 5's start (4.9 forecast). Of the added ones, the decision's wait is there three times (1.7 us; 2.2 forecast), and two short ones, 0.45, come with the list of tokens. The 2.4 us for `oL` were the wrong wait: not one shows. The gathers wait instead, 1.6 us, because TensorE is there for the second one 4.8 us after its request (588.32 to 593.11) and it takes 5.6. That the loads are as near to the edge as forecast is shown by gather_late and dw_gather, where they become late the moment the gathers do not; in no_keep neither is waited for.

**D, predicted 1.7 and 1.3 of clock, measured 2.9 and about 1.7.** The time at the tail fell to 3.53 instead of 4.7, for a reason that E had at nothing: the experts' partial reads (x_experts, 2.8 us). Tile by tile finishing is worth 1.1 (no_alone). The two are not to be added: against before's 6.42, the kernel with part 1 and without part 5 has 4.63, the one with part 5 and without part 1 in the experts 6.34, both together 3.53. So part 5 shows its worth only with part 1.

**E, predicted 0, measured 2.6 in the experts** beside the clock (271.0 to 266.7, less 1.7): 1.05 are idle time that is gone ([rows 1] 232.95 of 234.00, after 234.00 of 234.00). The remaining 1.6 were not traced to a line. x_blocks and x_experts show that part 1 does not carry them; no_keep (269.6) and no_spread (268.5) lose 2 to 3 us against after, gather_late 1.7. In no_keep 1.13 of that are one wait of TensorE for gathered rows, at 823.61, in no_spread 1.23 one wait for a decision, at 687.13; after has neither. That the order of the routing and the loads decides, and not one part, is likely, but not shown.

**A version that beats both:** dw_dve, 894.69, clearly faster than before. Against after it is 2.8 us lower in the median of four runs, with intervals that touch. From start to end its profile is 3.2 us shorter, of which 1.55 are a dip of the clock that did not come and that dw_gather, with the same edit, has; so the marks support a gain of 1.6 to 3.2 us over after.
